# A state-space layer on one core: B's head load doubled, the first two channel tiles interleaved, the warm-up made of wide matmuls

## The chip, the core and the metric

The kernel runs on one core of a Trainium2 chip. TensorE (PE) multiplies matrices into PSUM, VectorE (DVE) and ScalarE (ACT) work elementwise, GpSimd (POOL) fills constants and issues some transfers, SyncE (SP) issues most transfers. Each engine takes its own instructions in order and waits on semaphores for the others. The metric is the device time of the whole program in microseconds (us), a median over runs; lower is better. Beside it stands one profiled execution with its trace.

## The reference

With x of 2048 rows (time) by 1024 features, the output is `g * a + (1 - g) * b`, where `g` is a sigmoid of a row's dot product with `gate_w`, `a` is a diagonal complex state-space layer, and `b` is x with an update on eight selected rows:

```
Lam_bar = exp(dt * Lam);  B_bar = ((Lam_bar - 1) / Lam)[:, None] * (B_re + 1j * B_im)
Bu = einsum("bld,pd->blp", x, B_bar)
h[t] = Lam_bar * h[t-1] + Bu[t]                      # 1024 complex channels, 2048 steps
a = 2 * einsum("blp,dp->bld", h, C_re + 1j * C_im).real + x * Dskip
r = x @ w_r; idx = the 8 rows with the largest r
b = x, and at idx:  x + sigmoid(r) * ((silu(x @ w_gate) * (x @ w_up)) @ w_down)
out = g * a + (1 - g) * b
```

The two large products (x by B, h by C, real and imaginary plane each) are PE's work; the recurrence over time and the complex rotations around it are DVE's.

## The kernel before

Everything is in bf16 with sums in PSUM. `P` is 128 and `LC` is 256. Time is cut into 8 chunks `k` of 256 rows; two chunks form a block `m`, whose transposed input is `X[m]` (128 partitions, 8 feature tiles, 512 columns). The 1024 channels are 8 channel tiles `ct`.

**S1** (`s1u`, L274) multiplies for one block, one channel tile and one plane `pl` (0 real, 1 imaginary): 8 matmuls over the feature tiles, the weights a 128x128 piece of `BT[pl]`, the moving operand 512 columns of `X[m]`, or 256 when it is called for one chunk (`k0` to `k1`). The result stands in a PSUM tile `vps` of two banks, one for each plane; there are two such tiles. `s1e` (L281) copies both planes into SBUF as `V[k]`, one copy for each chunk, on ACT except for the very first channel tile, which DVE copies. Only the whole of a `vps` tile, both planes, is copied.

**DVE** then turns V by a table of angles (`dve_m`), scans it over time (`dve_scan0`), turns it back (`dve_post`) and gives `H[k]`. **S2** (L772, and L787 for the last 128 rows) multiplies H by `CT`. `add_upd` (L761), `fin_half` (L800) and the last L789 finish the last rows: the update of the eight rows (`yc`, L694) is added into the output in memory by an indirect transfer of POOL, then the last 256 rows are read back (`ul`, L758) and added on DVE.

The order on PE, DVE, ACT and SP is the order of the code; no scheduler moves anything there. At the beginning it is this. SP issues, one after another: one half of the first 256 rows as they are (`x0r`, the other half goes over ACT's queue), B's real tile 0 (`load_B(0, 0, 1)`), the second chunk of x transposed on the way (`load_xT(1)`), B's imaginary tile 0, and then B's tiles pair by pair, real and imaginary, the last two of each plane in one load. PE meanwhile multiplies zeros (`wt0`, L153, 14 matmuls of 256 columns, cleared by DVE in L85), transposes `x0r` itself (L164, copied out by DVE and ACT in L165 and L166), transposes three small vectors (L169), and starts S1 with channel tile 0: the real plane on the first chunk, the real plane on the second, two tiny matmuls (`vb_ps`, L404), and the imaginary plane on both at once. Then follows channel tile 1 in full, and so on. The buffer of `wt0` is later that of the tile `xsel32`, which POOL clears in L508 ahead of its two loads of `vrg`, the operand of L404.

On DVE the copies of the first `vps` tile stand behind the first half of the angle table (L212 to L220) and the small angles (L389 to L393), and ahead of everything else that DVE does.

Of the kernel before, what the change touches and what calls it, by code (L numbers as in the profile page):

```python
# [10 lines left out]
F32 = mybir.dt.float32  # L11
BF16 = mybir.dt.bfloat16
# [4 lines left out]
P = 128  # L17
LC = 256
# [6 lines left out]
def kernel(  # L25
# [39 lines left out]
    const = ctx.enter_context(tc.tile_pool(name="const", bufs=1))  # L65
    small = ctx.enter_context(tc.tile_pool(name="small", bufs=1))
    ps_s1 = ctx.enter_context(tc.tile_pool(name="ps_s1", bufs=2, space=PSUM))
    ps_s2 = ctx.enter_context(tc.tile_pool(name="ps_s2", bufs=2, space=PSUM))
    ps_m = ctx.enter_context(tc.tile_pool(name="ps_m", bufs=2, space=PSUM))
# [9 lines left out]
    def load_B(pl, c0, c1):  # L79
        nc.sync.dma_start_transpose(BT[pl][:, :, c0 * P:c1 * P], Bsrc[pl][c0 * P:c1 * P, :])  # L80

    load_B(0, 0, 1)
    vrow = small.tile([P, 3, P], BF16, name="vrow", tag="va")
    wt0 = small.tile([P, LC], BF16, name="wt0", tag="wt")
    nc.vector.memset(wt0[:], 0.0)  # L85
    nc.vector.memset(vrow[:], 0.0)
    for i, v in enumerate((A_log_dt, A_Lambda_re, A_Lambda_im)):
# [9 lines left out]
    def load_X(m):  # L97
        new_X(m)
        load_xT(2 * m)
        load_xT(2 * m + 1)  # L100
# [1 line left out]
    new_X(0)  # L102
    load_xT(1)
    load_B(1, 0, 1)
    for c0, c1 in ((1, 2), (2, 3), (3, 4), (4, 5), (5, 6), (6, 8)):
        for pl in range(2):
            load_B(pl, c0, c1)
    load_X(1)

    def load_C(pl, d0_):  # L110
# [8 lines left out]
    def big_new(name, k, shape=None, dt=BF16):  # L119
        want = {"V": "H", "U": "U", "H": "V", "D": "V"}[name]  # L120
        pick = next((e for e in big_free if e[1] == want), big_free[0])
        big_free.remove(pick)
        big_tag[name, k] = pick[0]
        return const.tile(shape or [P, 2, NCT, LC], dt, name=name, tag=pick[0])
# [21 lines left out]
    for i, v in enumerate((B_w_r, gate_w)):  # L146
        nc.gpsimd.dma_start(vrg[0:NCT, i, :], v.rearrange("(c p) -> c p", p=P))

    wps = ps_m.tile([P, LC], F32, name="wps", tag="m")

    def warm(n):
        for _ in range(n):
            nc.tensor.matmul(wps[:], lhsT=wt0[:, 0:P], rhs=wt0[:], start=True, stop=True)  # L153

    warm(14)
    vec = small.tile([P, 3, NCT], F32, name="vec")
    KH = KD // 2
    for tl in range(BPC):
        ts = slice(tl * P, (tl + 1) * P)
        xqa = ps_s2.tile([P, KH, P], BF16, name="xqa", tag="zps")  # L160
        pool, tag = (ps_m, "m") if tl else (ps_s1, "vps")
# [45 lines left out]
    def tab_arg(q):  # L207
        ur = const.tile([P, 2, QC, LC], F32, name="tu", tag="XP3")
        u, rn = ur[:, 0], ur[:, 1]
        for c in range(QC):  # L210
            ct = q * QC + c
            nc.vector.tensor_scalar(out=u[:, c, :], in0=ramp[:], scalar1=thp[:, ct:ct + 1], scalar2=None, op0=ALU.mult)  # L212
        nc.vector.tensor_scalar(out=rn, in0=u, scalar1=MAGIC, scalar2=MAGIC, op0=ALU.add, op1=ALU.subtract)
        f = tabp.tile([P, QC, LC], F32, name="tf", tag="tf", bufs=2)
        nc.vector.tensor_tensor(out=f[:], in0=u, in1=rn, op=ALU.subtract)
        tabs[q] = [f]
# [52 lines left out]
    def s1u(m, ct, pl, k0, k1):  # L269
        if (m, ct) not in vp:  # L270
            vp[m, ct] = ps_s1.tile([P, 2, 2, LC], F32, name="vps", tag="vps")
        o = vp[m, ct][:, pl, k0:k1, :].rearrange("p k t -> p (k t)")
        for dc in range(KD):
            nc.tensor.matmul(o, lhsT=BT[pl][:, dc, ct * P:(ct + 1) * P], rhs=X[m][:, dc, k0 * LC:k1 * LC], start=(dc == 0), stop=(dc == KD - 1))  # L274

    def s1e(m, ct, copy=nc.scalar.copy):
        for kk in range(2):
            k = 2 * m + kk
            if k not in V:
                V[k] = big_new("V", k)  # L280
            copy(out=V[k][:, :, ct, :], in_=vp[m, ct][:, :, kk, :])  # L281
        vp.pop((m, ct))

    def s1(m, ct):
        for pl in range(2):
            s1u(m, ct, pl, 0, 2)
        s1e(m, ct)
# [110 lines left out]
    nc.scalar.activation(out=trig[:, 0], in_=aab[:], func=ACT.Sin, scale=-TWO_PI, bias=halfpi[:])  # L398

    s1u(0, 0, 0, 0, 1)  # L400
    s1u(0, 0, 0, 1, 2)
    vb_ps = ps_m.tile([P, 2, NCT], F32, name="vb_ps", tag="m")
    for i in range(2):
        nc.tensor.matmul(vb_ps[:, i, :], lhsT=vrg[:, i, :], rhs=ident[:, 0:NCT], start=True, stop=True)  # L404
    s1u(0, 0, 1, 0, 2)
    s1e(0, 0, nc.vector.tensor_copy)
    tab_neg(0)
# [27 lines left out]
    nc.vector.tensor_scalar(out=rs4[:, 1, 1, :], in0=rot[:, 1, 1, :], scalar1=1.0, scalar2=None, op0=ALU.mult)  # L435
    nc.vector.tensor_scalar(out=rs4[:, 1, 0, :], in0=rot[:, 1, 1, :], scalar1=-1.0, scalar2=None, op0=ALU.mult)

    s1(0, 1)
    tab_arg(1)
    tab_abs(1)  # L440
    nc.vector.tensor_copy(rg[:, :, 0:2].rearrange("p k t -> p t k"), vb_ps[:])
# [513 lines left out]
```

## Time and profile before

| | |
|---|---|
| runs | 245.45, 246.24, 248.27 us; median 246.24 us |
| the profiled execution | 245.63 us, of which the span from the first to the last instruction is 243.9 us |
| PE | busy 238.1 us (98%), 1348 instructions |
| DVE | busy 227.9 us (93%), 234 instructions |
| ACT | busy 118.0 us (48%) |
| POOL | busy 30.4 us (12%) |

The profile's times start at the first instruction of the span, so 243.9 is its end. A busy time says how long an engine had something in work; the engine that the end waits for is read from the chain of waits, which goes back from the last instruction to what released it.

### The profile page before, as it was taken

To read this page: it belongs to the slowest core of one execution; us is meant where nothing else is said; L and a number is where in the kernel's file an instruction comes from. 1 tells how busy PE (TensorE), PEld (TensorE's weight loads), DVE (VectorE), ACT (ScalarE), POOL (GpSimd) and SP (SyncE) were. 2 spreads that over 40 slices of the span, in tenths; PEclk is the share of its full clock that TensorE was granted. 3 is DMA by queue.
4 is the path that set the end of the run, shared out by engine and by line. 5 is a ranking of instruction groups with operands and counts; after the bars stand their busy time and mean duration, and the time that the engine had idled before them with its cause. 6 is when DMAs were issued, how large, how long until landed. Compare 5 with 4: busy or idle time off the path is not lost.

```text
span 243.9 us, 3517 instructions
## 1 busy us (share of the span) xinstructions
PE 238.1 (98%) x1348; PEld 112.7 (46%) x1372; DVE 227.9 (93%) x234; ACT 118.0 (48%) x203; POOL 30.4 (12%) x50
## 2 busy tenths in 40 slices
PE   8899999999999999999999999999999999999995
PEld 6544444444444444444444444444444444446453
DVE  2899999999999999999999999999999999999964
ACT  3699973233653472323455462235267445456320
POOL 5000000000000500840002031000100211110120
PEclk9999999999999999999999999999999999999999
DMA  7999999997396260179347979686599999963054
GB/s 190 199 153 204 232 249 243 203 242 159 63 340 224 79 182 0 18 168 286 109 188 249 361 231 359 180 281 261 183 371 278 390 311 303 90 143 43 0 107 114
DMA packets 66425, 48.69 MB, mean 200 GB/s; under 512 B 51668, under 2 KB 53460, under 8 KB 66408
## 3 DMA queue, kind: packets, MB, share of 16 engines
q1 hardware_dynamic: 61192, 37.67, 58.4%
q0 software_dynamic: 3296, 7.38, 14.6%
q10 hardware_dynamic: 1920, 3.41, 4.0%
q8 instruction: 11, 0.18, 0.3%
q14 instruction: 6, 0.05, 0.1%
HBM read 27.55 MB, written 8.41 MB: 147 GB/s over the span
## 4 chain that ended last, share of the span: by engine, by line
PE 95%; DMA 2%; SPq 1%; issue 1%; DVE 0%
PE vps L274 45%; PE zps L772 42%; PE zps L787 3%; PE pgu L661 3%; DMA X<-in_A_x_dram 2%; PE y L673 1%; PE zr L487 1%; SPq L80 1%; SPq L77 0%; DVE ot L789 0%; PE vb_ps L404 0%; PE fl_ps L542 0%
## 5 line engine op out<-in xcount | busy, mean ns | idle before, releaser
L274 PE MATMUL vps<-X,BT 128*128 128x512 bf16 (+1 forms) x508 | 111.4, 376 | 1.3 <-DMA X<-in_A_x_dram 0.5
L772 PE MATMUL zps<-CT,H 128*128 128x512 bf16 x469 | 104.2, 379 | 0.6
L274 PEld LDWEIGHTS <-BT 128*128 128x128 bf16 x520 | 50.6, 98 | 60.8 <-PE pgu L661 1.1
L772 PEld LDWEIGHTS <-H 128*128 128x128 bf16 x480 | 46.6, 98 | 56.9 <-issue 1.3
L311 DVE TENSOR_TENSOR_SCAN U<-d,U 128x2048 bf16<-128x2048 f32 (+2 forms) x22 | 62.0, 2859 | 0.5
L281 ACT CAST V<-vps 128x512 bf16<-128x512 f32 x62 | 33.2, 587 | 56.7 <-PE vps L274 56.6
L777 ACT ACTIVATE ot<-zps,gcol 128x512 bf16<-128x512 f32 x30 | 20.6, 686 | 44.8 <-PE zps L772 42.6
L743 ACT CAST zps<-xd 128x512 f32<-128x512 bf16 (+2 forms) x30 | 16.7, 562 | 4.1 <-ACT xt L730 3.3
L301 DVE TENSOR_TENSOR V<-V,nTi 128x4096 bf16<-128x4096 bf16 (+2 forms) x11 | 16.7, 1516 | 0.5
L300 DVE TENSOR_TENSOR U<-V,T2tab 128x4096 bf16<-128x4096 bf16 (+2 forms) x11 | 16.6, 1509 | 0.5
L302 DVE TENSOR_TENSOR U<-U,V 128x4096 bf16<-128x4096 bf16 (+2 forms) x11 | 16.7, 1517 | 0.4
L707 POOL DMA_DIRECT2D xt<-in_A_x_dram x12 | 7.2, 598 | 77.1 <-DMA out_dram<-xt 38.7
L796 POOL DMA_DIRECT2D out_dram<-ot x14 | 13.1, 937 | 28.8 <-ACT ot L777 26.8
L336 DVE TENSOR_TENSOR U<-U,S2tab 128x4096 bf16<-128x4096 bf16 x7 | 16.0, 2292 | 0.2
L338 DVE TENSOR_TENSOR H<-H,U 128x4096 bf16<-128x4096 bf16 x7 | 16.0, 2293 | 0.2
L730 ACT ACTIVATE xt<-xt,omgcol 128x1024 bf16<-128x1024 bf16 x14 | 16.0, 1145 | 0.0
L334 DVE TENSOR_TENSOR H<-U,Ctab 128x4096 bf16<-128x4096 bf16 x7 | 16.0, 2284 | 0.0
L369 DVE TENSOR_TENSOR_SCAN U<-D,U 128x1024 bf16<-128x1024 f32 x4 | 8.9, 2280 | 0.1
L725 DVE TENSOR_TENSOR xd<-xt,Dbc 128x1024 bf16<-128x1024 bf16 x14 | 9.0, 684 | 0.0
L720 POOL DMA_DIRECT2D out_dram<-xt x2 | 1.5, 757 | 50.2 <-ACT zps L743 50.2
L661 PE MATMUL pgu<-wgu,xsel 128*32 128x448 bf16 x128 | 7.2, 354 | 0.0
L787 PE MATMUL zps<-CT,H 128*128 128x128 bf16 (+2 forms) x63 | 7.1, 271 | 0.1
(150 smaller groups left out, 131.7 us busy)
## 6 DMA issues: line engine op xcount, KB each, us to landing
wgu<-in_B_w_gate_dram SPq DMA_DIRECT2D x16, 448.0 KB, 4.6
wgu<-in_B_w_up_dram SPq DMA_DIRECT2D x16, 448.0 KB, 7.5
out_dram<-ot POOLq DMA_DIRECT2D x14, 256.0 KB, 5.9
wdb<-in_B_w_down_dram SPq DMA_DIRECT2D x7, 512.0 KB, 12.0
xt<-in_A_x_dram POOLq DMA_DIRECT2D x12, 256.0 KB, 4.1
out_dram<-xt ACTq DMA_DIRECT2D x12, 256.0 KB, 4.1
wd<-in_B_w_down_dram SPq DMA_DIRECT2D x5, 512.0 KB, 8.0
xt<-in_A_x_dram SPq DMA_DIRECT2D x4, 256.0 KB
```

Of the source, the lines that this page charges most:

```text
L274: nc.tensor.matmul(o, lhsT=BT[pl][:, dc, ct * P:(ct + 1) * P], rhs=X[m][:, dc, k0 * LC:k1 * LC], start=(dc == 0), stop=(dc == KD - 1))
L281: copy(out=V[k][:, :, ct, :], in_=vp[m, ct][:, :, kk, :])
L300: nc.vector.tensor_tensor(out=u, in0=v, in1=T2tab[:, :, c0:c1, :], op=ALU.mult)
L301: nc.vector.tensor_tensor(out=v, in0=v, in1=bc(nTi, c0, c1), op=ALU.mult)
L302: nc.vector.tensor_tensor(out=u, in0=u, in1=V[k][:, ::-1, c0:c1, :], op=ALU.add)
L311: nc.vector.tensor_tensor_scan(out=fl, data0=d0[:, c0:c1, :].rearrange("p c t -> p (c t)"), data1=fl, initial=0.0, op0=ALU.mult, op1=ALU.add)
L334: nc.vector.tensor_tensor(out=h, in0=g, in1=bc(Ctab, c0, c1), op=ALU.mult)
L336: nc.vector.tensor_tensor(out=g, in0=g, in1=S2tab[:, :, c0:c1, :], op=ALU.mult)
L338: nc.vector.tensor_tensor(out=h, in0=h, in1=G[k][:, ::-1, c0:c1, :], op=ALU.add)
L743: nc.scalar.copy(out=z[:], in_=xd[b][:, d_:d_ + w])
L772: nc.tensor.matmul(zps[:], lhsT=H[k][:, pl, ct, tl * P:(tl + 1) * P], rhs=CT[pl][:, ct, dsl], start=(fresh and ct == 0 and pl == 0), stop= ...
L777: nc.scalar.activation(out=ots[b][:, dsl], in_=zps[:], func=ACT.Copy, scale=gcol[:, b:b + 1])
```

## The change

Four edits, all at the kernel's beginning.

1. SP's first load of B brings the real tiles 0 and 1 in one transfer of 256 rows; after the second x chunk come the imaginary tiles 0 and 1 singly, then tiles 2 to 5 pair by pair; at the end the real tiles 6 and 7 singly and the imaginary 6 and 7 in one.
2. PE works channel tiles 0 and 1 together: the real plane of both on the first chunk, the two tiny matmuls, the real plane of both on the second chunk, the imaginary plane of tile 0, then, after some code for the other engines, that of tile 1.
3. The warm-up is 7 matmuls of 512 columns in place of 14 of 256.
4. `wt0` is twice as wide and lies in the buffer that `X[1]` takes later, no longer in that of `xsel32`.

```
-    load_B(0, 0, 1)
+    load_B(0, 0, 2)
-    wt0 = small.tile([P, LC], BF16, name="wt0", tag="wt")
+    wt0 = const.tile([P, 2 * LC], BF16, name="wt0", tag="XP1")
...
     load_xT(1)
     load_B(1, 0, 1)
-    for c0, c1 in ((1, 2), (2, 3), (3, 4), (4, 5), (5, 6), (6, 8)):
+    load_B(1, 1, 2)
+    for c0 in range(2, 6):
         for pl in range(2):
-            load_B(pl, c0, c1)
+            load_B(pl, c0, c0 + 1)
+    for pl, c0, c1 in ((0, 6, 7), (0, 7, 8), (1, 6, 8)):
+        load_B(pl, c0, c1)
     load_X(1)
...
-    wps = ps_m.tile([P, LC], F32, name="wps", tag="m")
+    wps = ps_m.tile([P, 2 * LC], F32, name="wps", tag="m")
-    warm(14)
+    warm(7)
...
     s1u(0, 0, 0, 0, 1)
-    s1u(0, 0, 0, 1, 2)
+    s1u(0, 1, 0, 0, 1)
     vb_ps = ps_m.tile([P, 2, NCT], F32, name="vb_ps", tag="m")
     for i in range(2):
         nc.tensor.matmul(vb_ps[:, i, :], lhsT=vrg[:, i, :], rhs=ident[:, 0:NCT], start=True, stop=True)
+    s1u(0, 0, 0, 1, 2)
+    s1u(0, 1, 0, 1, 2)
     s1u(0, 0, 1, 0, 2)
     s1e(0, 0, nc.vector.tensor_copy)
...
-    s1(0, 1)
+    s1u(0, 1, 1, 0, 2)
+    s1e(0, 1)
```

On SP's queue, the first seven rows (BT_72 is B's real plane, BT_73 the imaginary one, X_87 the second x chunk; the last number is the tile's size):

```order
 L77 DMA x0r<-in_A_x_dram 128x1024
-L80 DMA_TRANSPOSE BT_72<-in_A_B_re_dram 128x8x128
+L80 DMA_TRANSPOSE BT_72<-in_A_B_re_dram 128x8x256
 L95 DMA_TRANSPOSE X_87<-in_A_x_dram 128x8x256
-L80 DMA_TRANSPOSE BT_73<-in_A_B_im_dram 128x8x128
+L80 DMA_TRANSPOSE BT_73<-in_A_B_im_dram 128x8x128 x2
 L80 DMA_TRANSPOSE BT_72<-in_A_B_re_dram 128x8x128
```

The load of real tile 1 has moved from behind the second x chunk and imaginary tile 0 to ahead of both.

On PE, from the small vectors to the third channel tile, before (vps_214, vps_279 and vps_322 are the PSUM tiles of channel tiles 0, 1 and 2; a row for each run of matmuls of one form, of which there are 8 or, at 128x256 here, 16):

```order
L169 MATMUL va_ps_168<-ident_113,vrow_80 128x8
...
L274 MATMUL vps_214<-X0_87,BT0_72 128x256
...
L404 MATMUL vb_ps_231<-ident_113,vrg_124 128x8
...
L274 MATMUL vps_214<-X0_87,BT1_73 128x512
...
L274 MATMUL vps_279<-X0_87,BT0_72 128x512
...
L274 MATMUL vps_279<-X0_87,BT1_73 128x512
...
L274 MATMUL vps_322<-X0_87,BT0_72 128x512
```

And now, on the same engine and stretch (vps_207, vps_216 and vps_323 are those of channel tiles 0, 1 and 2; each row stands for 8 matmuls):

```order
L277 MATMUL vps_207<-X0_87,BT0_72 128x256
...
L277 MATMUL vps_216<-X0_87,BT0_72 128x256
...
L407 MATMUL vb_ps_225<-ident_113,vrg_124 128x8
...
L277 MATMUL vps_207<-X0_87,BT0_72 128x256
...
L277 MATMUL vps_216<-X0_87,BT0_72 128x256
...
L277 MATMUL vps_207<-X0_87,BT1_73 128x512
...
L277 MATMUL vps_216<-X0_87,BT1_73 128x512
...
L277 MATMUL vps_323<-X0_87,BT0_72 128x512
```

The 16 real-plane matmuls of channel tile 1 have moved ahead of the imaginary plane of tile 0, cut into halves of 256 columns. On DVE, ACT and POOL the instructions stand in the order in which they stood.

## Rows read from the trace of the kernel before

**Rows 1.** The chain that ended last, in order of time: start us, us, what.

```profile
1.20 1.31 SPq L80
2.57 5.22 DMA X<-in_A_x_dram
...
9.10 10.74 PE vps L274 x49
...
234.75 6.30 PE zps L787 x60
241.08 0.35 DVE ot L789
```

**Rows 2.** PE's instructions in order of time, its beginning: start, us, what, idle before.

```profile
1.06 3.17 PE L153 MATMUL wps<-wt 128*128 128x256 bf16 x14 [1.06 <-DVE wt L85]
...
5.82 0.27 PE L169 MATMUL va_ps<-ident,vrow 128*128 128x8 bf16 x3
6.11 1.24 PE L274 MATMUL vps<-X,BT 128*128 128x256 bf16 x8
7.83 1.03 PE L274 MATMUL vps<-X,BT 128*128 128x256 bf16 x8 [0.47 <-DMA X<-in_A_x_dram]
```

**Rows 3.** SP's queue in order of time, issues of B and x.

```profile
5.36 1.32 SPq L80 DMA_TRANSPOSE BT<-in_A_B_im_dram  x1
...
21.14 2.25 SPq L80 DMA_TRANSPOSE BT<-in_A_B_re_dram  x1
23.43 2.15 SPq L80 DMA_TRANSPOSE BT<-in_A_B_im_dram  x1
```

**Rows 4.** The issue of B's imaginary tile 0 at 5.36: median us from issue to landing.

```profile
BT<-in_A_B_im_dram SPq DMA_TRANSPOSE x1, 3.5
```

**Rows 5.** DVE's instructions in order of time, around its first copies of vps.

```profile
11.25 0.17 DVE L393 TENSOR_TENSOR afr<-ang,arn 128x16 f32<-128x16 f32 x1
11.34 1.28 DVE L281 CAST V<-vps 128x512 bf16<-128x512 f32 x2
```

**Rows 6.** All waits of DVE: waited for, us in total, times, longest.

```profile
DVE X L165 <- PE xqa L164: 4.0, 2, 3.6
DVE xt L761 <- DMA ul<-out_dram: 2.1, 1, 2.1
...
DVE ot L789 <- PE zps L787: 0.8, 1, 0.8
DVE ang L187 <- ACT dt_b L184: 0.5, 1, 0.5
```

**Rows 7.** DVE's instructions in order of time, the end.

```profile
229.69 0.53 DVE L694 TENSOR_SCALAR yc<-yc,rsel_c,omg 8x1024 bf16<-8x1024 bf16 x1 [0.19 <-DVE omg L600]
...
231.59 0.69 DVE L383 TENSOR_TENSOR H<-H,U 128x1024 bf16<-128x1024 bf16 x1
...
236.41 1.29 DVE L761 TENSOR_TENSOR xt<-xt,ul 128x1024 bf16<-128x1024 bf16 x2 [2.08 <-DMA ul<-out_dram]
237.80 0.76 DVE L800 TENSOR_TENSOR ot<-ot,xt 128x512 bf16<-128x512 bf16 x2
239.31 2.12 DVE L789 SCALAR_TENSOR_TENSOR ot<-zps,gcol,xt 128x512 bf16<-128x512 f32 x4 [0.75 <-PE zps L787]
```

**Rows 8.** Busy time in windows, L789 alone: window, length, DVE busy (instructions), granted clock, DMA.

```profile
239.00:242.00 3.00, 1.90 (x4) 1.00 0.46 150
```

**Rows 9.** PE's instructions in order of time, the last stage.

```profile
233.89 7.15 PE L787 MATMUL zps<-CT,H 128*128 128x512 bf16 x63
```

**Rows 10.** Busy time in windows, whole core: window, length, PE, PEld, DVE, ACT, POOL, granted clock, DMA.

```profile
4.00:6.00 2.00, 2.00 (x21) 1.87 (x20) 0.79 (x2) 0.58 (x1) 1.52 (x3) 1.00 1.26 261
```

**Rows 11.** ACT's and POOL's instructions in order of time, near the start.

```profile
6.06 0.58 ACT L166 COPY X<-xqb 128x512 bf16<-128x512 bf16 x1 [0.27 <-PE xqb L164]
...
15.27 1.04 ACT L281 CAST V<-vps 128x512 bf16<-128x512 f32 x2
...
4.29 0.31 POOL L508 MEMSET xsel<- 128x256 bf16 x1 [2.07 <-PE wps L153]
```

## The prediction

> **What bounds the kernel now.** I read the chain of waits first. It is PE's almost from end to end: before 9.10 us it goes through SP's first issues and the landing of the second x chunk, from 9.10 to the last matmul through matmuls alone, and it ends in one small DVE instruction [rows 1]. So PE never waits after 9.10, and a microsecond saved ahead of that point should be a microsecond saved, if no second engine stands close behind. The second view is DVE's waits, and there one does. DVE waits 4.0 us for the transposed rows and 0.5 us for ACT, all before 7 us, and then for nothing until the read-back `ul` near the end (2.1 us) and the last matmuls (0.8 us) [rows 6]. Between 7 and 234 us DVE is one unbroken row of work in fixed order: whatever delays it early arrives at the end undiminished.
>
> At the end the two chains lie close. DVE finishes `fin_half` at 237.80 + 0.76 = 238.56 and idles 0.75 us until PE has the first part of the last rows; its four L789 stretch over 2.12 us but work only 1.90, so 0.22 more is waiting [rows 7, 8]. DVE's slack against the end is thus about 0.97 us. One step earlier, the H of the first half of the last block is done at 231.59 + 0.69 = 232.28 and PE starts on it at 233.89: slack 1.6 us, a little less because the weights are loaded ahead [rows 7, 9].
>
> **The start as it is.** PE has the small vectors at 6.09, runs the first 8 half-width matmuls from 6.11 to 7.35, waits for the x chunk, which was issued at 2.57 and took 5.22 (7.79), and runs the next 8 from 7.83 [rows 1, 2]. The imaginary tile 0 was issued at 5.36 and landed 3.5 us later, 8.86 [rows 3, 4]; PE has its next full-width matmul at 9.10. From there a 512-column matmul costs (10.74 - 0.38)/48 = 0.216 us (49 in a row, of which the last is in work for 0.38) and a 256-column one half: the eight from 7.83 take 1.03, the last of them 0.27, so (1.03 - 0.27)/7 = 0.109. Channel tile 2 therefore starts at 9.10 + 24 x 0.216 = 14.28.
>
> **The head load and the x chunk.** SP needs 2.15 to 2.25 us to issue a 256-row load of B, against 1.31 for 128 rows [rows 1, 3]. The x chunk is then issued at 1.20 + 2.2 + 0.05 = 3.45 in place of 2.57, and lands 0.9 us later, at 8.7. The double load of B lands, if it takes what the x chunk of the same size took, at 1.20 + 5.22 = 6.4; by the bytes, somewhat later: half of `x0r`, the single tile and the x chunk, together 1024 KB on SP's queue, were there by 7.79; now 256 KB less stand ahead of this point, which at the 261 GB/s of that stretch [rows 10] is 1.0 us, so 6.8. I take 6.7, nearer to the slow end because `x0r` travels ahead of it. PE, ready at 6.09, so waits 0.6 us here. That is partly free: the second half of the operand comes from ACT's copy, which ends at 6.06 + 0.58 = 6.64 anyway [rows 11].
>
> **PE's sum.** First halves of tiles 0 and 1: 6.75 + 16 x 0.109 = 8.49. Two tiny matmuls, under 0.1. Second halves wait for x: 8.75 to 8.8, I take 8.8; they end at 10.54. The imaginary tile 0, issued at 3.45 + 2.75 + 0.05 = 6.25 and landing 3.5 later, is there at 9.8, the imaginary tile 1 at 11.1, needed at 12.3: neither waits. Channel tile 2 starts at 10.54 + 16 x 0.216 = 14.0. PE gains 14.28 - 14.0 = 0.3 us: it idles less because tile 1 fills the time in which it stood still for the x chunk, but the chunk itself is nearly a microsecond later. Bounds: if the loads come 0.5 us sooner 0.8, if 0.5 later a loss of 0.2.
>
> **DVE's sum.** DVE comes to the copies of the first `vps` at 11.34, directly behind L393, and waits for nothing [rows 5]. Now channel tile 0 is complete only after 16 + 16 half matmuls and the 8 of the imaginary plane: 10.54 + 8 x 0.216, plus the tail of the last one, 0.16, gives 12.43. DVE starts the copies at 12.47, and everything queued behind them on DVE, all of it down to the last block, starts 1.13 us later. Nobody else is hurt on the way: the copies last 1.28, so this PSUM tile is free at 13.75 and PE wants it at 14.0 for channel tile 2; ACT's copy of tile 1 starts at 15.27 behind its own work [rows 11], after the tile's end at 14.2. When PE is 0.3 early and DVE 1.13 late, the two move apart by 1.4 us, whatever the loads do, since DVE waits for PE; the 1.6 us at the last block still just covers that.
>
> **The end.** The scatter of `yc` and the read-back hang on DVE's L694, so `ul`, `fin_half` and the first L789 move by the same 1.13 us; the slack there is 0.97. The end comes 1.13 - 0.97 = 0.16 us later than before, though PE is done 0.3 us sooner. The sum against the profiled execution is 243.9 + 0.16 = 244.1 for the span, 245.63 + 0.16 = 245.8 for the time.
>
> **The edits that cost nothing.** The warm-up has the same 3584 columns, and its matmuls already ran without gaps (14 in 3.17 us, starts 0.21 us apart [rows 2]); clearing twice the zeros costs DVE perhaps 0.1 us ahead of it, and the wait for `x0r` behind it covers that. POOL no longer waits 2.07 us for the warm-up before it clears `xsel32` [rows 11], so `vrg` comes 2 us sooner; PE did not wait for it. `X[1]`'s load now waits for the warm-up, over by 4.3; SP reaches it after 25 us. The other loads of B keep their number and size, 12 single and 2 double; real tile 1 aside, each is issued within a load's length of its old place.
>
> **Rivals.** *The loads come early* (the double load at 6.3, the x chunk by 8.2): both sums shift by 0.6, PE gains 0.9, DVE loses 0.5, the end comes about 0.5 us sooner: 245.2 from the profiled time. For it: the queue is empty at the head; against it: SP's issue alone puts the chunk 0.9 us back. *The loads come late* by 0.5 us: the end comes 0.7 us later, 246.3. *PE's clock rises later*, the case on the slower side. The profile grants 1.00 in the window from 4 to 6 us [rows 10], but the warm-up's 256 columns take 0.21 us each, the pace of 1.2 GHz, and those after 7.83 take 0.109, that of 2.4; in between, at 6.11, the eight take 1.24, a mixture [rows 2]. So the clock rose in the very stretch in which PE will now stand idle for 0.6 us. If it rises only after 8.5, the 16 first half matmuls take 16 x 0.213 = 3.4 in place of 1.74 and end at 10.2, the second halves start 1.4 us later than reckoned, and so do PE and DVE: the end is 0.16 + 1.4 = 1.6 us later, 247.2 from the profiled time. Below 0.3 us of delay the wait for the x chunk swallows it. *The change does less than it says*: PE gains, but the end is DVE's; that is the forecast itself. Were DVE's delay to vanish somewhere on its way, the end would be PE's and come 0.3 us sooner, 245.3; the list of waits shows no place for it.
>
> The Trainium skill (TensorE: Matmul & The Clock Gate, Part 1: The HAM clock gate) says that the slow clock is the default, that sustained activity releases it, and that the moment is not tied to the kernel's start and differs from run to run. By that rule the late rise would come now and then in both kernels; the trace has a single execution and can't show it.
>
> **How the numbers follow.** Forecast (within 0.4 us of the 0.16): 0.55. Loads early: 0.2. Loads late: 0.12. Clock late: 0.13. The profiled execution is 0.6 us below the median of the three runs, so 0.16 later is 245.8 from the one and 246.4 from the other; I name 246.2. The range takes in the early case from the profiled time, 245.2, and the late clock from the median, 247.8. The three runs span 2.8 us, so about 1% (2.5 us) is what a measurement tells from no change. No case reaches it; I leave 0.05 for faster and 0.05 for slower, for what I have not seen.
>
> **What would show it.** After: SP's first issue of B about 2.2 us, the x chunk issued near 3.45; PE idle from 6.0 to about 6.7 and again from 8.5 to 8.8, then no more; channel tile 2 near 14.0; a new wait of DVE of about 1.1 us for PE ahead of its first copies of `vps`; at the end no wait of DVE for PE before L789, `ul` still waited for. A chain of waits that passes through DVE's late part would confirm the step on which all hangs. The forecast is wrong if DVE's new wait is much shorter, or if the end follows PE.

## The result, and the profile after

The changed kernel takes 248.58 us (median of 20 runs, 246.54 to 259.08) where the kernel before takes 246.0 (20 runs beside them, 245.3 to 248.27). The ratio, 1.0093 [1.0073, 1.0113], leaves out the four slowest runs of the change (250.28 to 259.08), and the 16 others have a median of 248.21, 2.2 us above before. The forecast was 246.2, at most 247.8. The profiled execution took 247.86 us, its span is 246.1; before these were 245.63 and 243.9.

PE's instructions at the beginning, changed kernel (they answer to [rows 2]):

```profile
5.50 0.63 PE L167 MATMUL xqb<-ident,x0r 128*128 128x128 bf16 x4
...
6.96 0.19 PE L172 MATMUL va_ps<-ident,vrow 128*128 128x8 bf16 x1 [0.79 <-DMA vrow<-in_A_Lambda_im_dram]
7.70 3.27 PE L277 MATMUL vps<-X,BT 128*128 128x256 bf16 x16 [0.56 <-DMA BT<-in_A_B_re_dram]
...
10.86 11.40 PE L277 MATMUL vps<-X,BT 128*128 128x256 bf16 x60
```

Three things are new. PE stands still twice, for one of the small vectors (0.79) and for the head load (0.56). The first real halves start at 7.70 instead of the reckoned 6.75. And these 16 matmuls take 3.27 us, 0.204 each, in place of the reckoned 1.74: almost the 0.21 of the warm-up, the lower of the clock's levels. There is no second idle piece ahead of 10.86, since the x chunk has been there for two microseconds.

SP's queue at the head and at the end, where it issues the last five stores of the output (to [rows 1, 3]), and then for two of its issues the median us from issue to landing (to [rows 4]):

```profile
1.20 2.98 SPq L80 DMA_TRANSPOSE BT<-in_A_B_re_dram  x1
4.23 2.51 SPq L95 DMA_TRANSPOSE X<-in_A_x_dram  x1
6.78 2.66 SPq L80 DMA_TRANSPOSE BT<-in_A_B_im_dram  x2
...
241.44 1.15 SPq L807 DMA_DIRECT2D out_dram<-ot  x2
242.70 1.36 SPq L798 DMA_DIRECT2D out_dram<-ot  x3
```

```profile
X<-in_A_x_dram SPq DMA_TRANSPOSE x1, 4.7
BT<-in_A_B_im_dram SPq DMA_TRANSPOSE x1, 3.2
```

The head load's issue takes 2.98, not 2.2; the chunk, issued at 4.23, lands at 8.93, and the imaginary tile 0, issued in the row from 6.78, takes 3.2, near the 3.5 of before.

DVE's instructions around its first copies (to [rows 5]), its end (to [rows 7]), and then its longest waits (to [rows 6]):

```profile
12.13 0.18 DVE L396 TENSOR_TENSOR afr<-ang,arn 128x16 f32<-128x16 f32 x1
14.53 1.29 DVE L284 CAST V<-vps 128x512 bf16<-128x512 f32 x2 [2.22 <-PE vps L277]
...
240.99 0.76 DVE L806 TENSOR_TENSOR ot<-ot,xt 128x512 bf16<-128x512 bf16 x2
241.67 1.75 DVE L795 SCALAR_TENSOR_TENSOR ot<-zps,gcol,xt 128x512 bf16<-128x512 f32 x4
```

```profile
DVE X L168 <- PE xqa L167: 4.0, 2, 3.5
DVE V L284 <- PE vps L277: 2.2, 1, 2.2
DVE xt L767 <- DMA ul<-out_dram: 2.1, 1, 2.1
DVE vec L173 <- PE va_ps L172: 1.0, 1, 1.0
```

Against before, the list has two new waits: 2.2 for the first `vps`, 1.0 for the small vectors. It has lost one, that of 0.8 for the last rows of PE. The copies start 14.53 - 11.34 = 3.19 later, and `fin_half` ends at 240.99 + 0.76 = 241.75, again 3.19 later than 238.56: nothing on the 227 us between them takes up a part of it. PE's last stage and the chain of waits (to [rows 9] and [rows 1]):

```profile
235.88 7.15 PE L793 MATMUL zps<-CT,H 128*128 128x512 bf16 x64
```

```profile
...
241.75 1.31 DVE ot L795 x3
...
243.07 0.35 DVE ot L795
```

The end is DVE's: the four L795 follow `fin_half` with no gap and work 1.75 (1.90 before, [rows 8]). The chain as the profile follows it begins only at 240.90, inside `fin_half`, so that DVE's delay goes back to the first copies is read from the 3.19 at both places and tested in e6. The last starts at 243.07 instead of 241.08, 1.99 later; PE's last stage, at 235.88 instead of 233.89, is 1.99 later too. So both engines carry the delay.

A last step stands behind DVE's: the stores, which the prediction left out. SP's queue at the end of the kernel before was this:

```profile
238.25 0.82 SPq L801 DMA_DIRECT2D out_dram<-ot  x2
240.09 1.73 SPq L792 DMA_DIRECT2D out_dram<-ot  x3
```

Between the two stores of `fin_half` and the three of the last rows SP was free for a microsecond. Now the five stand back to back from 241.44, the last issue is over at 242.70 + 1.36 = 244.06 instead of 241.82, 2.24 later, and that is the 2.2 of the span.

**The granted clock run by run.** In the profiled execution the column of the granted clock reads 1.00 throughout, in the slow stretch too, as it did during the warm-up before [rows 10]; there the pace is the only witness. Other runs have a mean granted clock of 0.993 over the execution: 8 of the 16 that the ratio rests on. The profiles of e1 and e11 below have that mean, and in both the clock fell for a stretch after it had risen. The eight take 248.19 to 249.8 us (median 248.8); the eight at 0.998 and above 246.54 to 250.05 (median 247.6). Since the profiled execution is one of the latter and slow all the same, a mean of 1.00 doesn't say that a run kept the higher pace: it counts falls, and not a late rise.

### The profile page after: what moved, and what is told of

Same layout as the page of the kernel before. It is cut to its first block, busy times and chain, and to the rows that moved or that the text cites. A ratio compares the mean times of both kernels' runs of the same rounds, so it can differ in the third digit from the quotient of the medians.

```text
span 246.1 us, 3544 instructions
## 1 busy us (share of the span) xinstructions
PE 240.5 (98%) x1373; PEld 113.0 (46%) x1373; DVE 227.9 (93%) x234; ACT 118.6 (48%) x203; POOL 30.3 (12%) x50
## 5 line engine op out<-in xcount | busy, mean ns | idle before, releaser
L277 PE MATMUL vps<-X,BT 128*128 128x512 bf16 (+1 forms) x528 | 113.1, 376 | 0.6 <-DMA BT<-in_A_B_re_dram 0.6
L277 PEld LDWEIGHTS <-BT 128*128 128x128 bf16 x528 | 51.8, 99 | 60.6 <-PE pgu L667 1.1
```

## The experiments

Theory L: the head load, with its long issue, is late, and PE and the rest only follow. Theory C: the idle of PE ahead of 7.70 costs it the higher clock. Theory D: what counts at the end is that DVE waits for tile 0, whose imaginary plane now comes only behind the real plane of tile 1. "After" is the changed kernel, "before" the one before it; each ratio is against before, run on the same chip.

| run | edit | us (before) | ratio |
|---|---|---|---|
| e1_double_load | before, new order of B's loads | 248.33 (245.84) | 1.0117 [1.0078, 1.0157] |
| e2_split_head | after, head load in two | 246.62 (245.84) | 1.0033 [1.0016, 1.0050] |
| e3_bridge | after, 4 matmuls in PE's gap | 247.19 (245.84) | 1.0063 [1.0040, 1.0087] |
| e4_wide_warm | before, new warm-up | 245.83 (245.84) | 0.9998 [0.9972, 1.0024] |
| e5_split_old_order | e2, PE's old order | 247.22 (245.89) | 1.0061 [1.0040, 1.0082] |
| e6_dve_fill | e2, DVE work moved into its wait | 245.93 (245.89) | 0.9997 [0.9978, 1.0017] |
| e7_order_only | before, PE's new order | 250.03 (245.89) | 1.0183 [1.0157, 1.0209] |
| e8_no_warm | before, warm-up of 1 matmul | 246.00 (245.89) | 1.0001 [0.9988, 1.0014] |
| e9_planes | both planes of tile 0 first | 245.98 (245.92) | 0.9989 [0.9966, 1.0012] |
| e10_bridge_fill | e3 and e6's DVE edit | 246.63 (245.92) | 1.0024 [1.0006, 1.0043] |
| e11_fill_only | after and e6's DVE edit | 248.46 (245.92) | 1.0098 [1.0069, 1.0128] |

**e1_double_load.** The new order of B's loads alone, with PE's old order and the old warm-up:

```
-    load_B(0, 0, 1)
+    load_B(0, 0, 2)
```

(and the order of the other loads as in the change).

> The kernel before with the new order of B's loads alone (real tiles 0 and 1 in one load at the head); PE's order and the warm-up are the old ones. Three theories of the 2.3 us that the change lost. Clock: PE idles from 6.1 until the double load lands near 7.7, so its clock rises only near 10.5, and the first 16 half-width matmuls run mostly 0.213 us apart; channel tile 2 starts near 16.0 and the end comes about 1.8 us later than before, nearly all of the loss without any change of PE's order. Load alone: the head load's lateness costs 1.6 us at the first matmul but the x chunk, 1.1 us later than before, sets the second half; with the clock at its upper level by then the end comes about 1.0 us later. Order: the loss comes from working two tiles together, so this kernel loses at most 0.5 us.

It was +2.5 where C had +1.8: this one edit alone costs as much as the whole change. Its parts are not quite the same: with the old order PE idles 0.63 for the chunk, and at the end it is DVE that waits for PE (1.3). PE's instructions from the small vectors on, and the windows with their granted clock, third figure from the end:

```profile
6.47 0.18 PE L172 MATMUL va_ps<-ident,vrow 128*128 128x8 bf16 x1 [0.70 <-DMA vrow<-in_A_Lambda_re_dram]
7.45 0.18 PE L172 MATMUL va_ps<-ident,vrow 128*128 128x8 bf16 x1 [0.80 <-DMA vrow<-in_A_Lambda_im_dram]
7.79 1.26 PE L277 MATMUL vps<-X,BT 128*128 128x256 bf16 x8 [0.16 <-DMA BT<-in_A_B_re_dram]
9.67 1.86 PE L277 MATMUL vps<-X,BT 128*128 128x256 bf16 x8 [0.63 <-DMA X<-in_A_x_dram]
```

```profile
6.00:8.00 2.00, 0.57 (x4) 0.40 (x5) 0.18 (x2) 0.55 (x2) 0.00 (x0) 1.00 1.07 156
8.00:8.50 0.50, 0.50 (x7) 0.44 (x6) 0.34 (x3) 0.19 (x2) 0.00 (x0) 0.98 1.28 290
8.50:9.00 0.50, 0.50 (x4) 0.22 (x2) 0.50 (x3) 0.48 (x2) 0.00 (x0) 0.50 1.29 279
...
12.00:14.00 2.00, 2.00 (x11) 0.88 (x9) 1.24 (x5) 2.00 (x5) 0.00 (x0) 1.00 0.90 176
```

Here the clock had risen, fell to 0.50 at about 8.5, behind the idle pieces of 0.70, 0.80 and 0.16 and with PE at work again (the piece of 0.63 came after the fall), and was back at 1.00 by 12. C was right in kind but had the moment wrong: it is not only that the clock may rise late, it is taken back. Five of the six runs show 0.993 or 0.985.

**e2_split_head.** After, with the head load as two of one tile each:

```
-    load_B(0, 0, 2)
+    load_B(0, 0, 1)
+    load_B(0, 1, 2)
```

(and real tiles 6 and 7 in one load, so that the number of loads stays).

> The changed kernel with its double head load split into two single loads in the same place, ahead of the x chunk; everything else is as changed (the last real tiles 6 and 7 come in one load again). Clock theory: the first tile lands near 5.8, PE starts S1 near 6.1 without idling, the clock rises near 6.5, channel tile 0 is complete near 12.5, DVE waits about 1.1 us for it, and the end comes 0 to 0.4 us later than before. Load alone: the same start, and the same end. Order theory: the loss stays at 1.5 us or more, since tile 0 is still finished behind half of tile 1.

It was +0.8 where at most 0.4 was expected. SP's first row and its last stores, then PE's and DVE's instructions:

```profile
1.20 2.85 SPq L80 DMA_TRANSPOSE BT<-in_A_B_re_dram  x2
...
239.45 1.42 SPq L808 DMA_DIRECT2D out_dram<-ot  x2
240.97 1.36 SPq L799 DMA_DIRECT2D out_dram<-ot  x3
...
6.17 2.11 PE L278 MATMUL vps<-X,BT 128*128 128x256 bf16 x16 [0.20 <-DVE X L169]
8.91 9.46 PE L278 MATMUL vps<-X,BT 128*128 128x256 bf16 x51 [0.60 <-DMA X<-in_A_x_dram]
...
12.58 1.29 DVE L285 CAST V<-vps 128x512 bf16<-128x512 f32 x2 [1.28 <-PE vps L278]
...
239.00 0.76 DVE L807 TENSOR_TENSOR ot<-ot,xt 128x512 bf16<-128x512 bf16 x2
239.68 1.80 DVE L796 SCALAR_TENSOR_TENSOR ot<-zps,gcol,xt 128x512 bf16<-128x512 f32 x4
```

Two issues take 2.85 together, no more than the one of 512 KB in after (2.98), and PE works from 6.17. This is the start that the prediction had drawn: first halves ahead of the chunk, chunk at 8.9 (8.8 reckoned), copies at 12.58 (12.47 reckoned), DVE without a wait at the end. What is left, 0.8, is left to D, and most of it shows at the stores: DVE ends at 239.68 + 1.80 = 241.48, only 0.05 later than before, but SP is held by the two stores of the delayed `fin_half` until 240.87, and the three behind them, in a row, are over at 242.33 instead of 241.82. That is 0.51 of the 0.59 by which the profiled execution (246.22) is longer than that of before.

**e3_bridge.** After, with two matmuls on the warm-up's zeros ahead of the small vectors and two behind them, into a PSUM tile that nothing reads; they are work added, and feed nothing:

```
+    wps2 = ps_s2.tile([P, 2 * LC], F32, name="wps2", tag="zps")
+    def bridge(n):
+        for _ in range(n):
+            nc.tensor.matmul(wps2[:], lhsT=wt0[:, 0:P], rhs=wt0[:], start=True, stop=True)
+    bridge(2)
     va_ps = ps_m.tile([P, 3, NCT], F32, name="va_ps", tag="m")
...
+    bridge(2)
     nc.vector.tensor_copy(vec[:, 0:3, :], va_ps[:])
```

> The changed kernel with four more matmuls on zeros of 512 columns, two ahead of the small vectors and two behind them, in the time in which PE waits; the loads are untouched. Clock theory: PE is kept busy, the clock rises near 6.5 as before, the first S1 matmuls start near 7.7 but run 0.109 us apart, tile 0 is complete near 13.1 in place of 14.5, and the end comes 0.6 to 1.0 us later than before in place of 2.3. Load alone and order: nothing changes, the end stays 2.3 us later, or 0.2 more if the extra matmuls delay PE.

```profile
5.87 1.06 PE L174 MATMUL wps<-wt 128*128 128x512 bf16 x2
...
6.88 0.72 PE L174 MATMUL wps<-wt 128*128 128x512 bf16 x2
7.77 1.92 PE L285 MATMUL vps<-X,BT 128*128 128x256 bf16 x16 [0.16 <-DVE are L200]
```

PE comes to the tiles no earlier than in after (7.77 against 7.70), but the 16 first halves take 1.92 in place of 3.27, and none of the 9 runs is below a mean clock of 0.999. The end came 1.35 later than before by the medians, where C had 0.6 to 1.0 and after has 2.2; the intervals of the two ratios (1.0063 and 1.0093) overlap, so this run alone does not settle C. The pair e10 and e11 does. The profiled execution (248.4) is no guide to the end: it is the second slowest of the nine, and in it DVE waits once, late, for a load of x (`xd`, L739: 1.0 us), as in no other profile here.

**e4_wide_warm.** Before, with the new warm-up alone (`wt0` twice as wide in the buffer of `X[1]`, `warm(7)`).

> The kernel before with the warm-up of 7 matmuls of 512 columns alone, its zeros in the other buffer. All three theories: PE starts some 0.1 us later behind the longer clearing, and the end moves by less than 0.2 us. If it were slower by a microsecond, the form of the warm-up itself would hold the clock back.

Nothing, as the prediction had it.

**e5_split_old_order.** e2 with PE's old order (tile 0 whole, then tile 1).

> The kernel of e2 (two single loads of B at the head, wide warm-up) with PE's order of before: tile 0 is finished before tile 1 begins. It asks what working two tiles together is worth when the loads are the same. If the loads set the pace: PE waits for the x chunk until 8.9 and for the imaginary tile 0 until 10.1, with nothing to do between; channel tile 2 starts near 15.3, 1.0 us later than before, DVE waits 0.7 us, and the end comes about 1.0 us later than before (e2: 0.8). If the interleaving itself is what costs, through DVE's wait for tile 0, this kernel ends at most 0.5 us later than before.

```profile
8.75 1.03 PE L278 MATMUL vps<-X,BT 128*128 128x256 bf16 x8 [1.41 <-DMA X<-in_A_x_dram]
...
240.40 2.12 DVE L793 SCALAR_TENSOR_TENSOR ot<-zps,gcol,xt 128x512 bf16<-128x512 f32 x4 [1.31 <-PE zps L791]
```

It was +1.3 (about +1.1 in the four runs that kept the clock) where about 1.0 was expected. With the two real tiles at the head but the old order, PE idles 1.41 for the chunk and the end is PE's (wait of 1.31). So the new order does for PE what it is for: in e2 the same idle is 0.60. Two of six runs have the clock at 0.993; none of e2's 12 has.

**e6_dve_fill.** e2, with four instructions of DVE (L212 of before for the second half of the angle table, which depend on nothing that is late) moved from behind the first copies to ahead of them:

```
+    tab_u(1)
     s1e(0, 0, nc.vector.tensor_copy)
```

> The kernel of e2 with four DVE instructions (the first step of the second half of the angle table, 1.14 us, which needs nothing new) moved ahead of DVE's copies of channel tile 0; nothing else moves. If DVE's wait of 1.28 us is what reaches the end in e2: the wait is filled, DVE's later work starts 0.1 us later than before in place of 1.2, the end is PE's again, whose channel tile 2 starts near 14.1, and the time is 0 to 0.3 us below before. If the end is not DVE's, it stays 0.8 us above before.

```profile
7.45 1.05 PE L285 MATMUL vps<-X,BT 128*128 128x256 bf16 x8 [0.29 <-DMA BT<-in_A_B_re_dram]
...
11.17 1.13 DVE L218 TENSOR_SCALAR tu<-ramp,ang 128x256 f32<-128x256 f32 x4
12.60 1.29 DVE L292 CAST V<-vps 128x512 bf16<-128x512 f32 x2 [0.30 <-PE vps L285]
...
239.38 2.12 DVE L804 SCALAR_TENSOR_TENSOR ot<-zps,gcol,xt 128x512 bf16<-128x512 f32 x4 [0.76 <-PE zps L802]
```

D holds: the copies start when they did in e2 (12.60), but 1.13 of DVE's later work is already done, the wait for PE at the end is back, 0.76 as in before (0.75), and the 0.8 is gone. It is no gain over before (0.9997). The first row belongs to the head loads: real tile 1, the second of the two single loads, is there only at 7.4.

**e7_order_only.** Before's loads with PE's new order; real tile 1 comes last of the first four loads.

> The kernel before with PE's new order alone; all loads and the warm-up are the old ones. Tile 1's real weights come only near 10.3, so PE stands idle from 7.1 to 10.4, with no change of any load. If an idle PE loses its clock: the matmuls after 10.4 run at the lower pace for some time, channel tile 2 starts near 17.5 to 18 and the end comes 3.2 to 4.2 us later than before. If the clock's rise has nothing to do with PE's idling: they run 0.109 us apart, channel tile 2 starts near 16.5, and the end comes 2.2 to 2.6 us later (PE by 2.2, DVE by 2.5).

```profile
5.73 1.03 PE L274 MATMUL vps<-X,BT 128*128 128x256 bf16 x8 [0.15 <-DVE X L165]
9.99 1.05 PE L274 MATMUL vps<-X,BT 128*128 128x256 bf16 x8 [3.23 <-DMA BT<-in_A_B_re_dram]
```

+4.1, at the upper end. PE idles 3.23; the profiled execution (247.7) kept the clock, as the 1.05 shows, and lost 1.8. The three others, at 0.993 to 0.985, took 249.76, 250.31 and 251.31: at least 2.1 us for the clock alone. So even a gap of 3.23 did not cost the clock in one of the four runs; in three it did.

**e8_no_warm.** Before with `warm(1)` in place of `warm(14)`.

> The kernel before with 1 matmul on zeros in place of 14; nothing else. PE is idle until the rows land near 4.1. If early work brings the clock's rise: it comes later than 6.5, the first S1 matmuls run 0.213 us apart, and the end comes 0.5 to 1.5 us later than before. If the rise falls at a random moment whatever PE does: the end stays within 0.3 us of before.

The expected 0.5 to 1.5 did not come; the median is unchanged, as the rival had it that puts the rise at a random moment. The profiled execution, the slowest of the ten (246.63), shows what a late rise costs in the old order:

```profile
6.22 3.57 PE L274 MATMUL vps<-X,BT 128*128 128x256 bf16 x16
```

All 16 halves of tile 0 at the slow pace, with no idle for the chunk between them: the wait that before has there [rows 2] takes up a part, and 246.63 - 245.63 = 1.0 is left. PE had no idle behind the transposes here, and idled 2.79 ahead of them; the column reads 1.00 throughout, so that how many of the other nine rose late isn't recorded. What the run shows is that the 13 matmuls on zeros buy nothing in the median; that idle time behind them counts is shown by e10 and e11, which that rival does not explain.

**e9_planes.** Another order: real and imaginary tile 0 as single loads at the head, both planes of tile 0 on the first chunk, then both on the second, tile 1 whole behind them.

```
-    load_B(0, 0, 2)
+    load_B(0, 0, 1)
+    load_B(1, 0, 1)
...
     s1u(0, 0, 0, 0, 1)
-    s1u(0, 1, 0, 0, 1)
+    s1u(0, 0, 1, 0, 1)
```

> Another way to fill the wait for the x chunk: the head loads are the real and the imaginary tile 0, singly, then the x chunk; PE works both planes of tile 0 on the first chunk, then both on the second, then tile 1 whole as before. Wide warm-up as in e2. If the account of e2 holds: channel tile 2 starts near 14.1 as there, but tile 0 is complete near 10.8, DVE waits for nothing, and the end comes 0 to 0.3 us earlier than before (e2: 0.8 later). If DVE's wait was not the reason for e2's loss, this kernel loses as much as e2.

```profile
11.42 1.28 DVE L283 CAST V<-vps 128x512 bf16<-128x512 f32 x2
...
239.69 2.12 DVE L792 SCALAR_TENSOR_TENSOR ot<-zps,gcol,xt 128x512 bf16<-128x512 f32 x4 [1.06 <-PE zps L790]
```

DVE has no wait ahead of the copies, as in before, and the end is PE's. The time is before's. That fits D, from the other side: the two chunks still fill PE's wait, and DVE gets tile 0 in time.

**e10_bridge_fill** and **e11_fill_only.** After with e6's DVE edit, once with the bridge of e3 and once without it.

> The changed kernel with both remedies: the four bridging matmuls of e3 and the four DVE instructions of e6 ahead of DVE's copies. The double head load stays. If the loss has three parts (clock, DVE's wait, the late load): the clock is held, DVE's delay falls under its slack, and what is left is PE's own lateness behind the late load, channel tile 2 near 14.8 against 14.28: the end comes 0.4 to 0.7 us later than before (e3: 1.4). If e3's rest is not DVE's wait: it stays at 1.2 or more.

> The changed kernel with the four DVE instructions of e6 ahead of the copies, without the bridge. In the trace of the changed kernel both chains come 2.0 us late at the end: channel tile 2 starts 1.8 us late on PE, and DVE's copies 3.2 us late, of which its slack takes 1.0. Filling DVE's wait leaves PE's lateness: the end stays 1.7 to 2.2 us later than before. If DVE alone set the end, it comes down to 1.0 or less.

e10 came as expected, e11 at 2.4 to 2.5, above its 2.2. PE and DVE of e10:

```profile
7.61 1.92 PE L292 MATMUL vps<-X,BT 128*128 128x256 bf16 x16 [0.39 <-DMA BT<-in_A_B_re_dram]
...
239.86 2.12 DVE L811 SCALAR_TENSOR_TENSOR ot<-zps,gcol,xt 128x512 bf16<-128x512 f32 x4 [0.85 <-PE zps L809]
```

And PE of e11:

```profile
5.07 0.39 PE L167 MATMUL xqb<-ident,x0r 128*128 128x128 bf16 x4
...
6.89 0.42 PE L172 MATMUL va_ps<-ident,vrow 128*128 128x8 bf16 x2 [1.42 <-DMA vrow<-in_A_Lambda_re_dram]
7.90 3.56 PE L284 MATMUL vps<-X,BT 128*128 128x256 bf16 x16 [0.58 <-DMA BT<-in_A_B_re_dram]
```

With the bridge the halves run in 1.92 and what is left is 0.6 to 0.7, the late head load on PE (its wait for it is 0.39 behind the bridge). Without it, four transposes in 0.39 show the clock up at 5 us (0.63 in after's profile, where it was not); then PE idles 1.42 and 0.58, and the 16 halves take 3.56. The intervals are apart: 1.0024 [1.0006, 1.0043] against 1.0098 [1.0069, 1.0128], some 1.8 us for the clock once DVE is out of the way; in the two profiles the pace of the halves alone makes 3.56 - 1.92 = 1.64. And filling DVE without the clock gains nothing (1.0098 against 1.0093), since PE is as late as DVE.

Over all runs, a mean clock of 0.993 or less, that is a fall, is seen in 8 of 16 of after, 7 of 11 of e11, 5 of 6 of e1, 3 of 4 of e7, 2 of 6 of e5, against 0 of 9 in e3, 0 of 12 in each of e2, e4, e6, e9 and e10, 0 of 10 in e8, and 1 or 2 of 23 to 27 in the runs of before beside them. In their profiles PE of the first group stands idle for 1.35 us or more in all between its transposes and 10 us, in the second for at most 1.0. That is one execution of each, and no run varied the length of the idle by itself; late rises, as in the profiles of after and e8, are not in these counts.

## Why the prediction was wrong

**The step that failed: when the head load lands.** "I take 6.7", from the 5.22 of the x chunk and from the bytes ahead of it; PE took it at 7.70. Its issue was put at 2.15 to 2.25, from rows at 21 us, and took 2.98 (2.88 to 3.22 in e1, e3, e10 and e11) as the first on the queue. The trace of before had a nearer row, the x chunk of the same size:

```profile
2.57 2.75 SPq L95 DMA_TRANSPOSE X<-in_A_x_dram  x1
```

The landing is late by more than the issue is long, though: 6.36 from issue to landing in e10's chain, where the x chunk took 5.22 before. The bound "0.5 later" was too tight, at 0.95. e2 brings the same two tiles as two loads, and PE has what it needs by 6.17. The second tile of such a pair came at about 7.4 in e6, so two loads don't bring the 512 KB much earlier; they hand over the first half when it is there. The small vectors, which were not in the sum at all, were late beside the load as well (0.79 on PE, 1.0 on DVE).

**The second step: two rivals that are one.** "Loads late" (0.12) and "clock rises later" (0.13) were given as alternatives, with 0.7 and 1.6 us. They came together, and not by chance: the late load, with the small vectors late beside it, makes the idle (0.56 and 0.79) that costs the clock. That pace is lost, and its price, were right: the 16 halves took 3.27 where 3.4 was said. That the clock can also fall after it had risen (e1, e11) was not seen; to the time it does the same. In 1 or 2 of some 25 runs it falls in the kernel before as well, in 8 of 16 after, so how often the kernel is hit hangs on PE's idle. The Trainium skill (TensorE: Matmul & The Clock Gate, Part 1: The HAM clock gate) has the moment of the rise differ from run to run. These runs bear that out: up to there after and e11 are the same on PE, and four transposes take 0.63 at 5.50 in the one and 0.39 at 5.07 in the other. The range ended where the clock's case alone ended, 247.8, and so left out their sum, which by the prediction's own terms (246.24 + 0.16 + 0.5 + 1.4) is 248.3.

**The rest of the working held.** With the two measured terms put in, the prediction's own sum comes out. The load costs PE 0.95 (7.70 for 6.75) and the pace 1.37 (3.11 from the first half to the next instruction at 10.81, for 1.74), less the 0.3 for which PE was to wait for the chunk. PE has the second halves at 10.86 instead of 8.8, 2.06 later; DVE's copies are reckoned at 12.47 + 2.06 = 14.53 and measured at 14.53; the delay passes undiminished to `fin_half` (3.19 at either place); 2.06 and the 0.16 of the end give 245.63 + 2.22 = 247.85, and the profiled execution is 247.86. The last agreement is closer than it deserves: DVE's slack was 3.19 - 1.99 = 1.2 in place of 0.97, mostly since the L795 take 1.75 where before they stretch over 2.12, and SP's stores added 2.24 - 1.99 = 0.25.

**DVE's wait** costs what was said of it and something more. e2 and e6 confirm the mechanism: where nothing is late and the clock stays, the change still costs 0.8, through this wait, and the cost goes when the wait is filled. The prediction had 0.16 for it, from DVE's own slack; the term it left out, put at nothing without a word, is SP's queue at the end, where the late `fin_half` stores push the last three (0.51 in e2).

**Warm-up, POOL, ACT, imaginary tiles**: nothing, as said (e4; no wait for POOL, ACT or the imaginary tiles in PE's rows).

**Where the 2.2 to 2.3 us lie**, from e10, e3 and after: about 0.6 to 0.7 is the late head load on PE, 0.6 (by medians, e3 to e10; 1.0 by ratios) DVE's wait, and the rest, 0.7 by ratios and 0.9 by medians, the clock. The last two overlap: without the clock's loss alone (e3) 0.7 to 0.9 comes back, without DVE's wait alone (e11) nothing, without both (e10) 1.5 to 1.7, since they delay two engines whose ends lie close. No version tried beats before by more than its interval.

**Open.** Why the three loads of 2 KB on ACT's queue come some 0.7 to 1.5 us later when the head load is one of 512 KB (e1, e10, e11 and after; not in e2, e5, e6): the traces show it, but no run varied those loads alone. Nor does a run show why that load takes a microsecond longer from issue to landing than the x chunk of the same size. And in after's profiled execution, whether the clock rose late or fell can't be read from the clock column; the slow transposes at 5.50 (0.63), and a column that shows no fall where those of e1 and e11 do, speak for a late rise there.

## What to carry to other kernels

A load that is merged at the head of a queue is ready as a whole, and late as a whole: where the first consumer needs only its first half, two loads issued in the same time here and let it start 1.5 us earlier. When a sum contains an idle of the matmul engine at the start, price the delay and the clock together, not as two alternatives: here the one brought the other in at least half of the runs. And before a second engine gets its first result later, ask what it could do meanwhile: here its slack at the end was one microsecond, the store queue behind it had less, and in e6, where nothing else was late, four instructions moved ahead of the wait gave all of it back.

## What was not expected of the hardware

- The clock was taken back after it had risen: in e1 granted 1.00 at 6 to 8 us, 0.50 from 8.5 with PE at work, 1.00 at 12 to 14. In e7 the runs in which it fell took 2.1 us or more longer than the one in which it did not.
- The granted-clock column read 1.00 from 8 to 10 us of after, while 256 columns took 0.204 us; the pace tells the level where the column does not.
- A transposing load of 256 rows took 2.88 to 3.22 us to issue as the first on its queue, 2.02 to 2.75 in other places (the x chunk among them); two of 128 rows in the same place 2.85 to 3.00 together.
- Taking away 13 of 14 warm-up matmuls changed nothing in the median: 1.0001 [0.9988, 1.0014].
